# Splitting the odd maximum tile over both row halves, and exponentials over pairs of PSUM banks, in a fused attention and token-mixing kernel

## The chip, the cores and the metric

The kernel runs on one core of a Trainium2 chip. A core has five engines with queues of their own: TensorE (PE in the profile; its weight loads are shown apart as PEld), VectorE (DVE), ScalarE (ACT), GpSimd (POOL) and SyncE (SP, which only issues DMAs here). They meet through semaphores. Matmul results land in PSUM, which has eight banks of 512 float32 values per partition; everything else lies in SBUF or DRAM. The metric is the time of one execution on the device in microseconds (us), of which the median over several runs is given.

## The reference

Two branches work on the same input x (2048 tokens, 640 channels, float32), and a gate per token mixes them. What the change touches is the attention branch with 32 heads of width 20:

```python
qkv = (x @ wqkv).reshape(B, S, 3, H, Dh)            # transposed to q, k, v per head
scores = jnp.einsum("bhqd,bhkd->bhqk", q, k) * (Dh ** -0.5)
p = softmax(scores, axis=-1)
a = (jnp.einsum("bhqk,bhkd->bhqd", p, v) back to (B, S, D)) @ wo

h = layernorm(x)                                     # branch B: MLP over the token axis
u = gelu(jnp.einsum("bsd,sf->bdf", h, w1) + b1)
b = (jnp.einsum("bdf,fs->bds", u, w2) + b2) transposed to (B, S, D)

g = sigmoid((x * gate_w).sum(-1, keepdims=True))
out = g * a + (1 - g) * b
```

All of it has to hold to float32 accuracy, so most products are made of two rounded parts, high and low, in three matmuls.

## The kernel before

Heads are worked on in 16 pairs p. Head j of a pair (j = 0, 1) has its rows of q and k stacked in partitions 64j to 64j + 61, so a matmul of head 0 uses the upper 64 rows of the PE array and one of head 1 the lower 64 rows; the two row halves can work side by side.

The softmax needs the maximum over all 2048 keys of each query before the exponentials are made. So each pair is gone through twice. The first pass (the "s" tiles, line 178) computes scores with queries as output partitions, 128 queries by 512 keys, and DVE reduces each tile to one maximum per query (line 180). There are 128 such tiles per pair: two halves of the queries, eight blocks t of 128 queries, four blocks kc of 512 keys, two heads. When the tiles of a half are done, `s_max` reduces the four partial maxima (line 143), negates and splits them on POOL, and `s_store` transposes and stores them to DRAM; `load_m` brings them back as two more rows of the q stack. The second pass (the "st" tiles, line 700) computes the scores again, with keys as output partitions and with the negated maximum added by those rows. ACT makes the exponential (line 703), and "pv" matmuls (line 637) multiply it by v.

The stages are: projections; the MLP of branch B, between whose matmuls the first 736 maximum tiles are spread (the loop that calls `s_next`); the attention loop; and the output projection (lines 724 to 750).

The attention loop has 16 x 32 iterations. An iteration takes 128 keys (kt) and 1024 queries (qh) of a pair: four st tiles (head j, column block c), four exponentials, and the pv products of the iteration before (`pv_flush`). Between the st matmuls it deals out the remaining 1312 maximum tiles, `take` of them, three in 344 iterations, two in 140 and none in the last 28. The variable `turn` alternates the heads so that an st tile in one row half stands next to an s tile in the other. With three s tiles there are seven tiles of 512 columns for two row halves. After the last pv product of 16 iterations, DVE copies the accumulated pv tile out of PSUM (`pv_evac`, line 618), and POOL issues its stores.

The order on every engine is the order of the program here: scheduling is switched to manual for PE, ACT and DVE, and later for POOL and SP. An instruction that waits therefore holds back all that stand behind it on its engine.

PSUM is divided by tags: "st" has four buffers of one bank, "s" three and "pv" one, eight banks in all. Buffers of a tag are used in turn: a new tile lands in the buffer of the tile that many places before it and has to wait until that tile was read. Exponentials land in twelve SBUF tiles of 512 columns ("pt").

Of the kernel before, what the change touches and what calls it, by code (L numbers as in the profile page):

```python
# [7 lines left out]
F32 = mybir.dt.float32  # L8
F32R = mybir.dt.float32r
AF = mybir.ActivationFunctionType  # L10
OP = mybir.AluOpType
AX = mybir.AxisListType

P = 128
S, D, H, DH, F = 2048, 640, 32, 20, 1728
# [13 lines left out]
def gated_mix(ctx, tc, xT, x, wqk, wv0, wv1, wo, w1, w1t, b1, w2, b2, out):  # L29
    nc = tc.nc  # L30
    EG = mybir.EngineType
    ctx.enter_context(tc.manual_schedule(engines={EG.PE}))
    PSUM = bass.MemoryType.PSUM
    SCALE = DH ** -0.5

    def hi_lo(hi, lo, src, hi_eng=None, lo_eng=None):
        if hi_eng is nc.scalar:
            nc.scalar.activation(hi, src, AF.Copy)  # L38
        else:
            (hi_eng or nc.vector).tensor_copy(hi, src)  # L40
        (lo_eng or nc.vector).tensor_sub(lo, src, hi.bitcast(F32))  # L41
# [22 lines left out]
    cp = ctx.enter_context(tc.tile_pool(name="cp", bufs=1))  # L64
    base = ctx.enter_context(tc.tile_pool(name="base", bufs=1))
    psum = ctx.enter_context(tc.tile_pool(name="psum", bufs=1, space=PSUM))

    def st_tile(shape, name):
        return psum.tile(shape, F32, tag="st", bufs=4, name=name)

    def s_tile(shape, name):
        return psum.tile(shape, F32, tag="s", bufs=3, name=name)
# [44 lines left out]
    def base_stack(p, full, eng=nc.sync):  # L117
        ks = k8([P, S], F32R, f"ks{p}_{full}")
        qs = [q4([P, S // 2], F32R, f"qs{p}_{full}_{i}") for i in range(2)]
        load_stack(p, ks, qs, full, eng)  # L120
        return ks, qs

    def load_m(p, qs, half, put=nc.sync.dma_start):
        src = m_d[p, half].rearrange("(g i j t) r -> i j t g r", i=2, j=2, t=8)
        for j in range(2):
            for i in range(2):
                r = 64 * j + 3 * DH + i
                dst = qs[half].bitcast(F32)[r: r + 1, :].rearrange("o (t g r) -> o t g r", g=4, r=32)
                put(dst, src[i: i + 1, j])

    s_src, st_src, v_tiles = {}, {}, {}

    def load_v(p):
        v_tiles[p] = base.tile([P, NT, NPAIR], F32, tag="v", bufs=2, name=f"v{p}")
        c0 = NPAIR * (p % 8)
        nc.sync.dma_start(v_tiles[p], v_d[p // 8, :, :, c0: c0 + NPAIR].rearrange("t p c -> p t c"))

    s_close = []

    def s_max(p, half, mx):  # L140
        mm = cp.tile([P, 16], F32, tag="mm", bufs=2, name=f"mm{p}_{half}")
        mc = cp.tile([P, 32], F32R, tag="mc", bufs=2, name=f"mc{p}_{half}")
        nc.vector.tensor_reduce(mm, mx.rearrange("p k j t -> p (j t) k"), axis=AX.X, op=OP.max)
        nc.gpsimd.tensor_scalar_mul(mm, mm, -1.0)
        hi_lo(mc[:, :16], mc[:, 16:], mm, hi_eng=nc.gpsimd, lo_eng=nc.gpsimd)
        s_close.append([8, lambda: s_store(p, half, mc)])

    def s_store(p, half, mc):
        mt = cp.tile([P, 32], F32, tag="mt", bufs=2, name=f"mt{p}_{half}")
        nc.vector.transpose(mt, mc.bitcast(F32))  # L150
        s_close.append([M_LAG[0], lambda: m_queue[0].dma_start(m_d[p, half], mt)])

    M_LAG = [8]

    def s_next():
        next(stream)()
        for e in list(s_close):
            e[0] -= 1
            if e[0] <= 0:
                s_close.remove(e)  # L160
                e[1]()

    def s_finish():
        next(stream, None)
        while s_close:
            s_close.pop(0)[1]()

    def s_tiles(p):
        for half in range(2):
            mx = cp.tile([P, 4, 2, 8], F32, tag="mx", bufs=2, name=f"mx{p}_{half}")  # L170
            for t in range(8):
                for kc in range(4):
                    for j in (1, 0):
                        def f(j=j, kc=kc, t=t):
                            ks, qs = s_src[p]
                            ps = s_tile([P, 512], f"s{p}_{half}_{t}_{j}_{kc}")
                            r = slice(64 * j, 64 * j + 3 * DH)
                            nc.tensor.matmul(ps, qs[half][r, t * P:(t + 1) * P], ks[r, kc * 512:(kc + 1) * 512],  # L178
                                             start=True, stop=True)
                            nc.vector.tensor_reduce(mx[:, kc, j, t: t + 1], ps, axis=AX.X, op=OP.max)  # L180
                        yield f
            s_close.append([2, lambda p=p, half=half, mx=mx: s_max(p, half, mx)])

    def s_stream(on_start):
        for p in range(NP):
            on_start(p)
            yield from s_tiles(p)

    hooks = [None]
    m_queue = [nc.gpsimd]  # L190
    stream = s_stream(lambda p: hooks[0](p))

    p1s = ExitStack()
# [99 lines left out]
    for half in range(2):  # L293
        wvh, wvl = wvs[half]
        width = HALF + 2 if half == 0 else HALF
        for t in range(NT):
            n = NT * half + t
# [9 lines left out]
            ps = st_tile([P, width], f"v{half}_{t}")  # L307
# [256 lines left out]
    while done < S_AHEAD:  # L564
        s_next()
        done += 1
# [5 lines left out]
    lp = lps.enter_context(tc.tile_pool(name="lp", bufs=1, side="right"))  # L572

    def s_stack(p):
        ks = lp.tile([P, S], F32R, tag="sk", bufs=2, name=f"sk{p}")
        qs = [lp.tile([P, S // 2], F32R, tag="sq", bufs=4, name=f"sq{p}_{i}") for i in range(2)]
        load_stack(p, ks, qs, False)
        return ks, qs
# [66 lines left out]
    def load_wo(c):  # L645
        raw = ap.tile([P, D], F32, tag="wor", bufs=1, name=f"wor{c}")
        nc.gpsimd.dma_start(raw, wo[c * P:(c + 1) * P, :])
        hi_lo(woh[c], wol[c], raw, hi_eng=nc.gpsimd, lo_eng=nc.gpsimd)
# [15 lines left out]
    def o_early(q, hi_eng=nc.scalar, lo_eng=nc.vector):  # L664
        o_hl[q] = o_part(q, slice(0, (NC - 1) * P), NC - 1, 256, "e", 2, hi_eng, lo_eng)
# [1 line left out]
    def o_late(q):  # L667
        return o_part(q, slice((NC - 1) * P, D), 1, 512, "l", 4, nc.scalar, nc.vector)[0]

    turn = given = 0  # L670
    LEFT = NP * 128 - S_AHEAD
    for p in range(NP):
        ks, qs = st_src[p]
        if 8 <= p < 8 + NC:
            load_wo(p - 8)
        for it in range(32):
            qh, kt = divmod(it, NT)
            if p + 1 < NP:
                if it == 6:
                    st_src[p + 1] = base_stack(p + 1, True)  # L680
                if it == 12:
                    load_v(p + 1)
                if it == 27:
                    load_m(p + 1, st_src[p + 1][1], 0)
            if it == 11 and p:
                load_m(p, qs, 1)
            if it == 14 and due_stack:
                n = due_stack.pop()
                if n < NP:
                    s_src[n] = s_stack(n)  # L690
            if p == NP - 1 and it in (20, 26):
                o_early(it // 26, nc.gpsimd, nc.gpsimd)
            if kt == 0:
                pv = psum.tile([P, 512], F32, tag="pv", bufs=1, name=f"pv{p}_{qh}")
            pts = {}

            def st_op(j, c, tile):
                r = slice(64 * j, 64 * j + 3 * DH + 2)
                ps = tile([P, 512], f"st{p}_{it}_{j}{c}")
                nc.tensor.matmul(ps, ks[r, kt * P:(kt + 1) * P], qs[qh][r, c * 512:(c + 1) * 512],  # L700
                                 start=True, stop=True)
                pt = lp.tile([P, 512], F32, tag="pt", bufs=12, name=f"p{p}_{it}_{j}{c}")
                nc.scalar.activation(pt, ps, AF.Exp, scale=SCALE)  # L703
                pts[j, c] = pt

            due = min((p * 32 + it + 1) * LEFT // (NP * 32 - 28) + 1, LEFT)
            take = min(due - given, 3)
            for n in range(4):
                st_op((n + turn) % 2, n // 2, s_tile if n == 2 and take < 3 else st_tile)
                if n < take:  # L710
                    s_next()
            given += take
            if take and given == LEFT:
                s_finish()
            turn = (turn + take) % 2
            pv_flush()
            if p * 32 + it in later:
                later.pop(p * 32 + it)()
            pend.append((p, qh, kt, pv, pts))
    pv_flush()  # L720
    ordered.close()
    lps.close()

    ep = ctx.enter_context(tc.tile_pool(name="ep", bufs=1, side="right"))
    tys = [ep.tile([P, 2, HALF], F32, name=f"oy{t}") for t in range(NT)]
# [13 lines left out]
    for t in range(NT):  # L739
# [5 lines left out]
        ps = [st_tile([P, HALF], f"a{t}_{i}") for i in range(2)]  # L745
        a_mms(t, ps, o_hl[t // 2], slice((t % 2) * P, (t % 2 + 1) * P), range(NC - 1))
    for t in range(NT):
        ps = [st_tile([P, HALF], f"b{t}_{i}") for i in range(2)]
# [49 lines left out]
```

## Time and profile before

| | |
|---|---|
| time, median of 3 runs | 1844.79 us (1844.1 to 1847.46) |
| span of the profiled execution | 1844.8 us |
| attention loop, first to last pv weight load | 702.1 to 1762.6 us |
| PE, DVE, ACT busy over the span | 99%, 77%, 74% |
| PE clock granted | 1.00 of full speed in the loop |

Rows of the groups read: line, engine, operation, output and input with their partitions and elements, number of instructions; then busy time in us and the mean duration of one in ns; then the idle time before them and what ended it. Rows of the timeline read: start in us, length in us from the first start to the last end of the merged instructions, engine, line, operation, number of instructions, and in brackets the idle time before them with what ended it. A PE matmul without weights loaded ahead starts, in the records, together with its weight load. Durations of neighbours on DVE and ACT overlap, so the distance between two starts tells how many fit into a time.

### The profile page before, as it was taken

How to read it: one execution, taken by the hardware profiler on the slowest of the kernel's cores; microseconds unless marked ns; L12 is line 12 of the kernel's file. 1: busy time of each engine (PE TensorE's matmuls, PEld its weight loads, DVE VectorE, ACT ScalarE, POOL GpSimd, SP SyncE). 2: the span in 40 equal slices, each digit the busy share in tenths (PEclk: the TensorE clock that was granted, in tenths of full speed). 3: DMA queues.
4: the chain of work that ended last, by engine and by line, in shares of the span. 5: the costliest groups of instructions: out<-in, count | busy, mean ns of one | idle time of the engine just before them, and what ended most of it. 6: DMA issues, size and time to landing. Idle time of an engine off the chain costs nothing. (4 is left out here: it accounts for less than half of the span.)

```text
span 1844.8 us, 39129 instructions
## 1 busy us (share of the span) xinstructions
PE 1829.7 (99%) x14978; PEld 1135.2 (62%) x14978; DVE 1428.9 (77%) x2341; ACT 1361.6 (74%) x2688; POOL 637.1 (35%) x900
## 2 busy tenths in 40 slices
PE   9999999999999999999999999999999999999998
PEld 7998799999999994333333333333333333333378
DVE  4202299999999998888888888888888888888137
ACT  4243244465444448999999999999999999999930
POOL 1013478888887770112112111121321211212210
PEclk9999999999999999999999999999999999999999
DMA  8456766566645645504032324213540423301463
GB/s 289 143 169 212 222 173 173 158 194 193 168 139 166 189 136 121 118 15 103 20 85 61 73 42 93 57 50 78 107 103 24 109 47 77 71 14 23 131 219 132
DMA packets 152831, 216.61 MB, mean 117 GB/s; under 512 B 65698, under 2 KB 92082, under 8 KB 148738
## 3 DMA queue, kind: packets, MB, share of 16 engines
q1 hardware_dynamic: 129172, 178.68, 35.4%
q0 software_dynamic: 14688, 20.78, 5.2%
q10 hardware_dynamic: 8784, 14.65, 2.4%
q8 instruction: 118, 1.93, 0.4%
q14 instruction: 69, 0.57, 0.1%
HBM read 165.43 MB, written 48.25 MB: 116 GB/s over the span
## 5 line engine op out<-in xcount | busy, mean ns | idle before, releaser
L180 DVE TENSOR_REDUCE mx<-s 128x1 f32<-128x512 f32 x2048 | 1293.7, 684 | 159.9 <-PE s L178 119.7
L703 ACT ACTIVATE p<-st 128x512 f32<-128x512 f32 x2048 | 1042.1, 615 | 20.9 <-PE s L178 2.2
L700 PEld LDWEIGHTS st<-qs_True,ks_True 62*128 62x128 f32 x2048 | 307.3, 185 | 485.1 <-ACT p L703 312.9
L700 PE MATMUL st<-qs_True,ks_True 62*128 62x512 f32 x2048 | 579.6, 425 | 0.2 <-ACT ty L477 0.2
L637 PE MATMUL pv<-p,v 128*32 128x512 f32 x4096 | 555.5, 605 | 0.2
L178 PE MATMUL s<-sk,sq 60*128 60x512 f32 x1280 | 423.1, 434 | 0.0
L41 POOL TENSOR_TENSOR wl<-wr,wh 128x512 fp32r<-128x512 f32 x228 | 273.6, 1216 | 59.8 <-ACT wh L38 30.9
L624 POOL DMA_DIRECT2D o_d<-oev x128 | 67.0, 524 | 494.3 <-DVE oev L618 491.6
L178 PE MATMUL s<-ks_False,qs_False 60*128 60x512 f32 x768 | 225.1, 397 | 0.4 <-DVE mx L180 0.3
L46 PE MATMUL y<-gh,wh 64*128 64x320 f32 x896 | 216.8, 308 | 0.0
L46 PE MATMUL y<-gl,wh 64*128 64x320 f32 x832 | 210.3, 306 | 0.0
L46 PE MATMUL y<-gh,wl 64*128 64x320 f32 x832 | 209.4, 305 | 0.0
L38 ACT ACTIVATE wh<-wr 128x512 fp32r<-128x512 f32 (+2 forms) x246 | 135.9, 594 | 90.2 <-PE s L178 29.0
L178 PEld LDWEIGHTS s<-sk,sq 60*128 60x128 f32 x1280 | 197.7, 185 | 1.2
L637 PEld LDWEIGHTS pv<-p,v 128*32 128x32 f32 x4096 | 84.9, 108 | 171.4 <-issue 156.4
L46 PE MATMUL u<-hl,wh 64*128 64x320 f32 x864 | 167.1, 306 | 0.0
L46 PE MATMUL u<-hh,wh 64*128 64x320 f32 x864 | 167.1, 306 | 0.0
L46 PE MATMUL u<-hh,wl 64*128 64x320 f32 x800 | 156.9, 306 | 0.4 <-POOL wl L41 0.4
L46 PEld LDWEIGHTS y<-gh,wh 64*128 64x128 f32 x896 | 155.3, 184 | 0.4
L46 PEld LDWEIGHTS y<-gh,wl 64*128 64x128 f32 x832 | 147.0, 184 | 0.3
L46 PEld LDWEIGHTS y<-gl,wh 64*128 64x128 f32 x832 | 146.9, 184 | 0.0
L178 PEld LDWEIGHTS s<-ks_False,qs_False 60*128 60x128 f32 x768 | 124.4, 184 | 1.1 <-DVE mx L180 1.1
(124 smaller groups left out, 1817.6 us busy)
## 6 DMA issues: line engine op xcount, KB each, us to landing
wr<-in_w_dram SPq DMA_DIRECT2D x196, 256.0 KB
ks_True<-k_d SPq DMA_DIRECT2D x96, 160.0 KB
qs_True<-q_d SPq DMA_DIRECT2D x192, 80.0 KB
sk<-k_d SPq DMA_DIRECT2D x60, 160.0 KB
sq<-q_d SPq DMA_DIRECT2D x120, 80.0 KB
v_d<-vt SPq DMA_DIRECT2D x32, 168.0 KB
v<-v_d SPq DMA_DIRECT2D x16, 336.0 KB
xr<-in_xT_dram SPq DMA_DIRECT2D x20, 256.0 KB
```

The source lines that it names most:

```text
L38: nc.scalar.activation(hi, src, AF.Copy)
L41: (lo_eng or nc.vector).tensor_sub(lo, src, hi.bitcast(F32))
L46: nc.tensor.matmul(ps[k], a[r], b[r], start=start, stop=stop)
L178: nc.tensor.matmul(ps, qs[half][r, t * P:(t + 1) * P], ks[r, kc * 512:(kc + 1) * 512], start=True, stop=True)
L180: nc.vector.tensor_reduce(mx[:, kc, j, t: t + 1], ps, axis=AX.X, op=OP.max)
L624: nc.gpsimd.dma_start(o_d[DH * h: DH * h + DH, cols], ev[r: r + DH, :])
L637: nc.tensor.matmul(pv[r: r + 32, :], v_tiles[p][:, kt, 10 * j: 10 * j + 32], pts[j, c], start=(kt == 0), stop=(kt == NT - 1))
L700: nc.tensor.matmul(ps, ks[r, kt * P:(kt + 1) * P], qs[qh][r, c * 512:(c + 1) * 512], start=True, stop=True)
L703: nc.scalar.activation(pt, ps, AF.Exp, scale=SCALE)
```

## The change

- The odd third s tile of an iteration is replaced by two tiles of 128 queries by 256 keys, one of each head, of the same query and key block. Head 0's is the iteration's first matmul, head 1's the last one ahead of pv. They are halves (h = 0, 1) of the key blocks kc = 2 and 3; another iteration takes the other half. Full tiles of kc = 0 and 1 that are passed over on the way are taken later (`s_skipped`).
- The maxima therefore have six places per query instead of four. A full tile of kc = 2 or 3 is reduced as two segments of 256 in one instruction, in the MLP stage too. `s_max` reduces six values in place of four.
- The two full s tiles of an iteration stand together between the two st pairs; the order of heads is fixed (`turn` is gone).
- In the loop the four st banks become two tiles of two banks ("sp"): one for each column block c, with both heads side by side. One exponential covers both banks, 1024 columns, and writes a pt tile of 1024 (six buffers). In an iteration with an odd number of s tiles the first pair (c = 0) is still made by two exponentials of 512.
- The st pool is closed ahead of the loop and opened again behind it.

The number of s buffers stays at three.

```diff
-        next(stream)()
+        if not s_one:
+            s_one.extend(s_full(s_skipped.pop(0) if s_skipped else next(stream)))
+        s_one.pop(0)()
+        s_tick()
...
+    def s_full(u):
+        def f(j):
+            ps = s_tile([P, 512], f"s{u.p}_{u.half}_{u.t}_{j}_{u.kc}")
+            u.mm(ps, j, 0, 512)
+            if u.kc < 2:
+                nc.vector.tensor_reduce(u.mx[:, u.kc, j, u.t: u.t + 1], ps, axis=AX.X, op=OP.max)
+            else:
+                nc.vector.tensor_reduce(u.mx[:, 2 * u.kc - 2: 2 * u.kc, j, u.t],
+                                        ps.rearrange("p (a b) -> p a b", a=2), axis=AX.X, op=OP.max)
+            u.ended(2)
+        return [lambda j=j: f(j) for j in (1, 0)]
+
+    def s_half():
+        while not s_rest:
+            u = next(stream)
+            if u.kc < 2:
+                s_skipped.append(u)
+            else:
+                s_rest.extend([(u, 0), (u, 1)])
+        u, h = s_rest.pop(0)
+
+        def f(j):
+            ps = s_tile([P, 256], f"s{u.p}_{u.half}_{u.t}_{j}_{u.kc}_{h}")
+            u.mm(ps, j, 256 * h, 256)
+            nc.vector.tensor_reduce(u.mx[:, 2 * u.kc - 2 + h, j, u.t: u.t + 1], ps, axis=AX.X, op=OP.max)
+            u.ended(1)
+
+        f(0)
+
+        def close():
+            f(1)
+            s_tick()
+
+        return close
...
+            sps = [pair_pool.tile([P, 2, 512], F32, tag="sp", bufs=2, name=f"st{p}_{it}_{c}") for c in range(2)]
+
+            def st_mm(c, j):
                 r = slice(64 * j, 64 * j + 3 * DH + 2)
-                ps = tile([P, 512], f"st{p}_{it}_{j}{c}")
-                nc.tensor.matmul(ps, ks[r, kt * P:(kt + 1) * P], qs[qh][r, c * 512:(c + 1) * 512],
+                nc.tensor.matmul(sps[c][:, j], ks[r, kt * P:(kt + 1) * P], qs[qh][r, c * 512:(c + 1) * 512],
                                  start=True, stop=True)
-                pt = lp.tile([P, 512], F32, tag="pt", bufs=12, name=f"p{p}_{it}_{j}{c}")
-                nc.scalar.activation(pt, ps, AF.Exp, scale=SCALE)
-                pts[j, c] = pt
+
+            def st_exp(c, apart):
+                pt = lp.tile([P, 2, 512], F32, tag="pt", bufs=6, name=f"p{p}_{it}_{c}")
+                for j in (slice(1, 2), slice(0, 1)) if apart else (slice(0, 2),):
+                    nc.scalar.activation(pt[:, j], sps[c][:, j], AF.Exp, scale=SCALE)
+                for j in range(2):
+                    pts[j, c] = pt[:, j]
...
-            for n in range(4):
-                st_op((n + turn) % 2, n // 2, s_tile if n == 2 and take < 3 else st_tile)
-                if n < take:
+            close = s_half() if take % 2 else None
+            for c in range(2):
+                for j in (1, 0):
+                    st_mm(c, j)
+                st_exp(c, close and c == 0)
+                if c == 0 and take > 1:
                     s_next()
+                    s_next()
+            if close:
+                close()
```

More of the change, by code (lines that the diff above doesn't have):

```diff
@@ L66, in gated_mix @@
     psum = ctx.enter_context(tc.tile_pool(name="psum", bufs=1, space=PSUM))
+    four = ExitStack()
+    banks = [four.enter_context(tc.tile_pool(name="four", bufs=1, space=PSUM))]
     def st_tile(shape, name):
-        return psum.tile(shape, F32, tag="st", bufs=4, name=name)
+        return banks[0].tile(shape, F32, tag="st", bufs=4, name=name)
     def s_tile(shape, name):
@@ L153, in gated_mix, with s_tick @@
     M_LAG = [8]
-    def s_next():
-        next(stream)()
+    def s_tick():
         for e in list(s_close):
@@ L161, in s_next @@
                 e[1]()
+    def s_next():
+        if not s_one:
+            s_one.extend(s_full(s_skipped.pop(0) if s_skipped else next(stream)))
+        s_one.pop(0)()
+        s_tick()
     def s_finish():
-        next(stream, None)
+        assert not s_one and not s_rest and not s_skipped
         while s_close:
             s_close.pop(0)[1]()
[L168 to L182, printed above, removed]
@@ new lines, in gated_mix, with __init__, mm, ended @@
+    s_one, s_rest, s_skipped = [], [], []
+    class Unit:
+        def __init__(self, p, half, t, kc, mx, left):
+            self.p, self.half, self.t, self.kc, self.mx, self.left = p, half, t, kc, mx, left
+        def mm(self, ps, j, lo, n):
+            ks, qs = s_src[self.p]
+            r = slice(64 * j, 64 * j + 3 * DH)
+            k0 = self.kc * 512 + lo
+            nc.tensor.matmul(ps, qs[self.half][r, self.t * P:(self.t + 1) * P], ks[r, k0: k0 + n], start=True,
+                             stop=True)
+        def ended(self, n):
+            self.left[0] -= n
+            if self.left[0] == 0:
+                s_close.append([2, lambda: s_max(self.p, self.half, self.mx)])
@@ L186, in s_stream @@
             on_start(p)
-            yield from s_tiles(p)
+            for half in range(2):
+                mx = cp.tile([P, 6, 2, 8], F32, tag="mx", bufs=2, name=f"mx{p}_{half}")
+                left = [128]
+                for t in range(8):
+                    for kc in range(4):
+                        yield Unit(p, half, t, kc, mx, left)
     hooks = [None]
@@ L668, in o_late @@
         return o_part(q, slice((NC - 1) * P, D), 1, 512, "l", 4, nc.scalar, nc.vector)[0]
-    turn = given = 0
+    four.close()
+    pairs = ExitStack()
+    pair_pool = pairs.enter_context(tc.tile_pool(name="pairs", bufs=1, space=PSUM))
+    given = 0
     LEFT = NP * 128 - S_AHEAD
@@ L695, in gated_mix @@
             pts = {}
-            def st_op(j, c, tile):
+            sps = [pair_pool.tile([P, 2, 512], F32, tag="sp", bufs=2, name=f"st{p}_{it}_{c}") for c in range(2)]
+            def st_mm(c, j):
                 r = slice(64 * j, 64 * j + 3 * DH + 2)
-                ps = tile([P, 512], f"st{p}_{it}_{j}{c}")
-                nc.tensor.matmul(ps, ks[r, kt * P:(kt + 1) * P], qs[qh][r, c * 512:(c + 1) * 512],
+                nc.tensor.matmul(sps[c][:, j], ks[r, kt * P:(kt + 1) * P], qs[qh][r, c * 512:(c + 1) * 512],
                                  start=True, stop=True)
-                pt = lp.tile([P, 512], F32, tag="pt", bufs=12, name=f"p{p}_{it}_{j}{c}")
-                nc.scalar.activation(pt, ps, AF.Exp, scale=SCALE)
-                pts[j, c] = pt
+            def st_exp(c, apart):
[4 more added lines that the diff above has]
+                    pts[j, c] = pt[:, j]
             due = min((p * 32 + it + 1) * LEFT // (NP * 32 - 28) + 1, LEFT)
             take = min(due - given, 3)
-            for n in range(4):
-                st_op((n + turn) % 2, n // 2, s_tile if n == 2 and take < 3 else st_tile)
-                if n < take:
+            close = s_half() if take % 2 else None
[4 more added lines that the diff above has]
+                if c == 0 and take > 1:
                     s_next()
+                    s_next()
+            if close:
+                close()
             given += take
@@ L714, in gated_mix @@
                 s_finish()
-            turn = (turn + take) % 2
             pv_flush()
@@ L721, in gated_mix @@
     ordered.close()
+    pairs.close()
     lps.close()
+    banks[0] = ctx.enter_context(tc.tile_pool(name="late", bufs=1, space=PSUM))
     ep = ctx.enter_context(tc.tile_pool(name="ep", bufs=1, side="right"))
```

## The prediction

> **What bounds the kernel now.** I read the page's engine totals first, then its costliest groups, then the same groups over 900 to 1700 us (the middle of the attention loop), and then single iterations in the timeline.
>
> ```profile
> span 1844.8 us, 39129 instructions
> PE 1829.7 (99%) x14978; PEld 1135.2 (62%) x14978; DVE 1428.9 (77%) x2341; ACT 1361.6 (74%) x2688; POOL 637.1 (35%) x900
> ...
> L703 ACT ACTIVATE p<-st 128x512 f32<-128x512 f32 x1540 | 785.4, 604 | 15.4 <-PE s L178 0.9
> L180 DVE TENSOR_REDUCE mx<-s 128x1 f32<-128x512 f32 x1044 | 660.4, 683 | 120.6 <-PE s L178 91.9 <-PE st L700 26.4
> ```
>
> The last two rows are of the 800 us window. 1540 exponentials are 385 iterations, so an iteration takes 2.078 us on average; 1044 maxima are 2.71 per iteration, that is 71% iterations with three maximum tiles ("threes") and 29% with two ("twos"). ACT looks full (785 of 800 us), DVE waits for PE for most of its idle time. Which engine really sets the period is seen in single iterations, here the PE rows of a three (from 1201.71), the start of the next, and of a two (from 1210.15):
>
> ```profile
> 1201.71 0.50 PE L700 MATMUL st<-qs_True,ks_True 62*128 62x512 f32 x1
> 1202.05 0.40 PE L700 MATMUL st<-qs_True,ks_True 62*128 62x512 f32 x1
> 1202.28 0.40 PE L700 MATMUL st<-qs_True,ks_True 62*128 62x512 f32 x1
> 1202.52 0.39 PE L700 MATMUL st<-qs_True,ks_True 62*128 62x512 f32 x1
> 1202.84 1.07 PE L637 MATMUL pv<-p,v 128*32 128x512 f32 x8
> 1203.84 0.49 PE L700 MATMUL st<-qs_True,ks_True 62*128 62x512 f32 x1
> 1203.84 0.50 PE L178 MATMUL s<-sk,sq 60*128 60x512 f32 x1
> ...
> 1210.15 0.50 PE L700 MATMUL st<-qs_True,ks_True 62*128 62x512 f32 x1
> 1211.05 1.07 PE L637 MATMUL pv<-p,v 128*32 128x512 f32 x8
> 1212.05 0.49 PE L700 MATMUL st<-qs_True,ks_True 62*128 62x512 f32 x1
> ```
>
> A three is four slots, each holding one matmul in either row half (score in one, maximum in the other): 0.34, 0.23, 0.24, 0.32, then pv 1.00; 2.13 in all. The first slot has 0.10 of weight loading that nothing hides, the last 0.09 to 0.10 of changing over to pv. In the fourth slot one row half is empty. A two is three slots and pv, 1.90. No step of either holds a wait: the loop is bound by PE's own sequence. From the average, a three is (2.078 - 0.29 x 1.90) / 0.71 = 2.15 us.
>
> ```profile
> 1204.37 1.09 ACT L703 ACTIVATE p<-st 128x512 f32<-128x512 f32 x2
> 1204.86 1.57 ACT L703 ACTIVATE p<-st 128x512 f32<-128x512 f32 x3
> 1202.55 1.87 DVE L180 TENSOR_REDUCE mx<-s 128x1 f32<-128x512 f32 x3
> 1203.74 1.35 DVE L180 TENSOR_REDUCE mx<-s 128x1 f32<-128x512 f32 x2
> 1204.40 1.29 DVE L180 TENSOR_REDUCE mx<-s 128x1 f32<-128x512 f32 x2
> ```
>
> ACT's exponentials start (1.57 - 0.60) / 2 = 0.48 apart though one lasts 0.60, so four need 1.92: the busy share overstates ACT, which has 0.2 to spare in a three and none in a two. DVE's maxima start (1.87 - 0.68) / 2 = 0.60 apart: three need 1.79.
>
> **The change, part by part.** From here "s1, s0" are the full maximum tiles of a three, "h0" and "h1" its two halves. The new PE order of a three is h0, score pair c=0, s1, s0, score pair c=1, h1, pv. There are 344 threes (1312 maxima to give out in 484 iterations: 344 x 3 + 140 x 2) and 140 twos, then 28 iterations without maxima.
>
> *Row halves.* Each half gets 3.5 tiles in place of 4 and 3. Whether a short matmul lets the next one of its half start early is told by the earlier MLP stage, where 320-column and 512-column matmuls mix:
>
> ```profile
> 450.03 0.30 PE L46 MATMUL y<-gh,wh 64*128 64x320 f32 x1
> 450.10 0.31 PE L46 MATMUL y<-gl,wh 64*128 64x320 f32 x1
> 450.17 0.39 PE L178 MATMUL s<-ks_False,qs_False 60*128 60x512 f32 x1
> 450.25 0.31 PE L46 MATMUL y<-gh,wl 64*128 64x320 f32 x1
> ```
>
> The starts alternate 0.07 to 0.08 apart, less than the 0.15 that one 320-column matmul takes in its half: the halves do run skewed. The Trainium skill, "TensorEngine Tiling (Array Packing)", Key Properties, says that different tiles can load weights and multiply in parallel; these rows agree. So, by PE alone, h1 could start 0.34 + 0.23 + 0.23 = 0.80 after the start, and pv 0.11 (256 columns at the 0.23 / 512 of a slot) and 0.10 later: 1.01 in place of 1.15. That is 0.14 x 344 = 48 us of gain, if nothing waits.
>
> *The wait that comes with it.* There are three s buffers, and a three now takes four: h0, s1, s0, h1. h1 therefore lands in the buffer of h0 of the same iteration, and PE must wait until DVE has reduced h0. Before, three tiles per iteration met a buffer that was a whole period old. When is h0 reduced?
>
> ```profile
> 1204.47 0.19 PEld L700 LDWEIGHTS st<-qs_True,ks_True 62*128 62x128 f32 x2 [0.34 <-DVE mx L180]
> 1204.91 0.16 PEld L637 LDWEIGHTS pv<-p,v 128*32 128x32 f32 x8 [0.25 <-issue]
> ...
> L618 DVE COPY oev<-pv 128x512 f32<-128x512 f32 x32 | 21.9, 683 | 39.9 <-PE pv L637 39.9
> L315 DVE COPY gs<-v 128x2 f32<-128x2 f32 x16 | 2.5, 159 | 28.9 <-ACT vt L312 28.9
> ```
>
> (1) First-slot maximum to its reduction: 1203.84 to 1204.40, 0.56; for 256 columns 0.11 less, 0.45. (2) The reduction of 256: copies from PSUM cost (683 - 159) / 510 = 1.03 ns per column, so 0.68 - 0.26 = 0.42. (3) Release to PE: the reduction from 1203.74 ended at 1203.74 + 0.68 = 1204.42 and the weight load that waited for it began at 1204.47: 0.05. So h1's weight load starts 0.92 after the iteration's start. (4) The weights of a matmul that waits are not loaded ahead: that pair of full width needed 1204.91 - 1204.47 = 0.44 to pv, a half 0.33. pv starts at 1.25 and the iteration ends at 2.25, in place of 2.15. **344 x 0.10 = +34 us.** The skew gives nothing back, as h1 is last before pv. Each of (1) to (4) is good to about 0.02, so the three lies between 2.20 and 2.28: +17 to +45. If h1 did not wait at all: -48.
>
> The Trainium skill, same page, Instruction Overhead, puts some 60 cycles on every matmul and so speaks against splitting one; at a column per cycle (0.43 ns, from 0.23 against 0.15 us for 512 against 320 columns) that is 0.026 us, by an estimate +9 us for 344 more matmuls if it were exposed. The same two rows leave 0.01 us per matmul, and here it disappears in the wait.
>
> *Evacuation of pv.* DVE copies pv every 16 iterations, 0.60 between starts, 0.24 after the next iteration's start:
>
> ```profile
> 1201.95 0.68 DVE L618 COPY oev<-pv 128x512 f32<-128x512 f32 x1
> ```
>
> Before, this delayed no matmul of that iteration (1201.71 to 1203.84 is 2.13). Now it holds DVE from 0.24 to 0.84, so h0's reduction starts at 0.84 instead of 0.45 and h1 comes 0.39 later. 30 evacuations fall among maxima, 71% of them into a three: **+8 us** (0 to +12).
>
> *Exponentials.* ACT's one 1024-wide shape is a copy from SBUF:
>
> ```profile
> L38 ACT ACTIVATE wh<-wr 128x512 fp32r<-128x512 f32 x196 | 116.0, 625 | 65.2 <-PE s L178 29.0 <-POOL ty L481 18.1 <-DMA wr<-in_w_dram 11.9
> L38 ACT ACTIVATE ohe<-ore 128x1024 fp32r<-128x1024 f32 x6 | 6.4, 1061 | 30.8 <-PE a L732 30.8
> ```
>
> The second 512 columns cost 0.44, against 0.48 for a separate exponential. A two falls from 1.92 to 1.84 of ACT, a three (whose first pair stays two instructions) to 1.88. PE needs 1.90 and 2.25, so this gains nothing: I take 0 (to -2 us). The price is that a pair's buffer comes free only after the whole 1.04 us exponential. After a two, pair c=1 is released 0.53 + 0.92 + 1.04 + 0.05 = 2.54 after that two's start, 0.64 into the next iteration, where PE would reach it at 0.57: with its weights it streams at 0.74, h1 could follow at 0.97, which is no later than the 1.02 that the wait for h0 gives already. Cost 0, and 0.17 x 140 = 24 us if that cover were gone.
>
> *Last 28 iterations.* They have no maxima and take 1.96 now:
>
> ```profile
> 1728.26 0.73 PE L700 MATMUL st<-qs_True,ks_True 62*128 62x512 f32 x4
> 1730.22 0.73 PE L700 MATMUL st<-qs_True,ks_True 62*128 62x512 f32 x4
> ```
>
> PE alone would need about 1.66, but with two pair buffers PE waits for each whole exponential in turn; I come to iterations between 1.7 and 2.2, on average about as before. 0 (-8 to +3).
>
> *Maxima in the MLP stage.* Half of the 736 early ones now reduce two segments of 256.
>
> ```profile
> 300.00:700.00 400.00, 393.66 (x626) 1.00 0.57 164
> L143 DVE TENSOR_REDUCE mm<-mx 128x16 f32<-128x64 f32 x32 | 8.1, 253 | 0.0
> ```
>
> These rows are L180's DVE time in that stage, and the only reduction with many segments. Its 253 ns are 159 and 64 x 1.03 = 66, and 28 over for 16 segments. One more segment costs 0 to 0.03 us; 313 of them are at most 9 us of DVE, against 400 - 626 x 0.60 = 24 us unclaimed between the starts. 0 (to +6). The last reduction over 6 in place of 4 partial maxima, the reopened PSUM pools (one drain each) and loads that start up to two units of work earlier: 0 to 2 us together; the DMAs are the same in number.
>
> Sum, against the profiled 1844.8 us (the median of the runs is 1844.79): +34 + 8 = +42, **1887 us**.
>
> **Rivals.**
> A, faster: h1 does not really wait. It decides at 0.82: if h0 is released 0.10 us earlier than (1) to (3) say, a three costs what it did, and 0.2 us earlier the full gain of the row halves comes in. Then 2.01 per three, 1844.8 - 48 = 1797. For it: the skewed rows at 450 us. Against it: the three measured terms would have to shrink by a tenth together for break-even, by a fifth for the whole gain.
> B, ACT becomes the bound: long exponentials don't overlap their successors. Then a two takes at least 2 x 1.04 = 2.08, +0.18 x 140 = 25, and the tail about 3 more: 1915. Against it: starts 0.48 apart at 0.60 each.
> C, the row halves don't overlap in the new order, so the change doesn't do what it says. A three keeps four slots, h1 could start at 0.80, still before 0.92: again 1887, with other rows in the trace.
> D, the wait is half of what I think: +0.04 x 344, 1844.8 + 14 = 1859, or break-even.
>
> **How the numbers follow.** My forecast with C has 0.79; A 0.11; B 0.05; D 0.05, of which 0.02 is no change. From no change a measurement of this kernel tells about 0.2%, 1841 to 1848.5. The range runs from the short end of the three without the evacuations (+17, 1862) to its long end with evacuations and MLP segments (+45 + 12 + 6, 1908). Slower 0.87, same 0.02, faster 0.11.
>
> **What the trace after would show.** Right: h1's weight load in a three waits for DVE, starting 0.92 after h0's; threes of 2.25, twos of 1.90; pv 0.33 after h1's load; ACT idle grows to 0.3 a three. Wrong: h1's matmul at 0.80 and threes near 2.0 (A); twos over 2.0 with PE waiting for ACT (B); a score matmul of c=0 starting with s1 only after both halves are empty (C). The prediction fails first if the reduction of 256 columns is much cheaper than 0.42, or if its release reaches PE before its recorded end.

## The result and the profile after

The changed kernel takes 1886.51 us (median of 4 runs, 1885.29 to 1888.32), the kernel before on the same chip 1844.44 us (1843.97 to 1847.46). The ratio is 1.0224, 95% interval 1.0206 to 1.0242: slower by about 42 us, where 1887 us was forecast.

The first rows are from the page of the changed kernel, the rows behind the dots from its groups over 900 to 1700 us, the window that the prediction used.

```profile
span 1884.6 us, 40589 instructions
PE 1860.4 (99%) x15322; PEld 1160.0 (62%) x15322; DVE 1458.7 (77%) x2685; ACT 1333.2 (71%) x2008; POOL 636.7 (34%) x900
...
L754 PE MATMUL st<-qs_True,ks_True 62*128 62x512 f32 x1484 | 393.3, 458 | 0.1
L217 DVE TENSOR_REDUCE mx<-s 128x1 f32<-128x256 f32 x527 | 220.7, 419 | 66.7 <-PE s L185 65.7
L185 PEld LDWEIGHTS s<-sk,sq 60*128 60x128 f32 x1268 | 179.2, 185 | 261.7 <-DVE mx L198 134.1 <-DVE mx L200 71.3 <-DVE mx L217 20.8
L200 DVE TENSOR_REDUCE mx<-s 128x2 f32<-128x512 f32 x240 | 155.3, 687 | 20.8 <-PE s L185 20.8
```

1484 score matmuls in 800 us are 371 iterations, 2.156 us each; before it was 2.078. PE's busy share is 99% in both, which again says nothing: while one matmul waits inside an iteration, the records of its neighbours cover the time. The row of the weight loads of s tiles shows a wait that was not there, for the halves' maxima (L217, 20.8 us); the longer times behind L198 and L200 are mostly pv standing between the s tiles of two iterations. A reduction of two segments costs 687 ns where the one of a single segment cost 683 to 685, so the MLP stage kept its length: its last matmul starts at 698.5 us, before at 698.2.

Now one three (from 1204.82) and the two behind it (from 1207.03) in the timeline of the changed kernel, PE and its weight loads first, then DVE and ACT (the last row names the form of its first exponential; its second is the 1024-wide one of c=1):

```profile
1204.82 0.38 PE L185 MATMUL s<-sk,sq 60*128 60x256 f32 x1
1204.82 0.61 PE L754 MATMUL st<-qs_True,ks_True 62*128 62x512 f32 x2
1205.16 0.51 PE L185 MATMUL s<-sk,sq 60*128 60x512 f32 x2
1205.72 0.18 PEld L185 LDWEIGHTS s<-sk,sq 60*128 60x128 f32 x1
1206.03 0.16 PEld L686 LDWEIGHTS pv<-p,v 128*32 128x32 f32 x8
1207.03 0.49 PE L754 MATMUL st<-qs_True,ks_True 62*128 62x512 f32 x2
1207.59 0.19 PEld L754 LDWEIGHTS st<-qs_True,ks_True 62*128 62x128 f32 x2 [0.27 <-ACT p L760]
1208.02 0.16 PEld L686 LDWEIGHTS pv<-p,v 128*32 128x32 f32 x8 [0.24 <-issue]
1209.02 0.38 PE L185 MATMUL s<-sk,sq 60*128 60x256 f32 x1
...
1205.24 0.42 DVE L217 TENSOR_REDUCE mx<-s 128x1 f32<-128x256 f32 x1 [0.24 <-PE s L185]
1205.53 1.09 ACT L760 ACTIVATE p<-st 128x512 f32<-128x512 f32 x2 [0.20 <-PE st L754]
1206.03 1.51 ACT L760 ACTIVATE p<-st 128x512 f32<-128x512 f32 x2
```

In the three, h0 is issued at 1204.82, DVE reduces it from 1205.24 to 1205.66, h1's weights are loaded at 1205.72, pv starts at 1206.03 and the iteration ends after 2.21 us. In the two, no s tile waits; but the weights of its c=1 pair are loaded only at 1207.59, 0.56 after its start, when the wide exponential of the three before (the second of the last row, which ends at 1206.03 + 1.51 = 1207.54) has let go of that pair's banks. pv follows at 0.99 instead of 0.90, and the two takes 1.99 instead of 1.90.

An evacuation of pv, in the three that starts at 1219.83:

```profile
1219.97 0.69 DVE L667 COPY oev<-pv 128x512 f32<-128x512 f32 x1
1220.58 0.41 DVE L217 TENSOR_REDUCE mx<-s 128x1 f32<-128x256 f32 x1
1221.05 0.18 PEld L185 LDWEIGHTS s<-sk,sq 60*128 60x128 f32 x1 [0.47 <-DVE mx L217]
1222.36 0.18 PEld L754 LDWEIGHTS st<-qs_True,ks_True 62*128 62x128 f32 x2 [0.84 <-ACT p L760]
```

The copy holds DVE when h0 is ready; h1 is loaded 1.22 after the start (1219.83) in place of 0.90, and this three takes 2.53 us.

From the starts of the first matmul of every iteration in the two traces come the means (in brackets the medians) in us; the first two iterations, threes, and the last one are left out:

| | before | after | iterations x difference of means |
|---|---|---|---|
| threes | 2.149 (2.132) | 2.231 (2.207) | 342 x 0.082 = 28.0 |
| twos | 1.913 (1.896) | 1.980 (1.987) | 140 x 0.067 = 9.4 |
| last ones, without maxima | 1.952 (1.961) | 2.023 (2.016) | 27 x 0.071 = 1.9 |

Together 39.3 of the 39.8 us between the two profiled spans (the medians of the runs are 42 us apart). The 21 threes with an evacuation last 2.53 on average and the others 2.21, where both took 2.15 before. Of the threes' 28.0, 342 x 0.06 = 21 are thus what every three pays, and 21 x 0.32 = 7 what the evacuations add.

### The profile page after: what moved, and what is told of

Read it like the earlier page. It is cut to its first block, busy times and chain, and to the rows that moved or that the text cites. A ratio compares the mean times of both kernels' runs of the same rounds, so it can differ in the third digit from the quotient of the medians.

```text
span 1884.6 us, 40589 instructions
## 1 busy us (share of the span) xinstructions
PE 1860.4 (99%) x15322; PEld 1160.0 (62%) x15322; DVE 1458.7 (77%) x2685; ACT 1333.2 (71%) x2008; POOL 636.7 (34%) x900
## 5 line engine op out<-in xcount | busy, mean ns | idle before, releaser
L760 ACT ACTIVATE p<-st 128x512 f32<-128x512 f32 (+1 forms) x1368 | 1013.3, 810 | 88.3 <-PE st L754 66.3
L198 DVE TENSOR_REDUCE mx<-s 128x1 f32<-128x512 f32 x1024 | 659.4, 685 | 52.1 <-PE s L185 50.3
L754 PE MATMUL st<-qs_True,ks_True 62*128 62x512 f32 x2048 | 540.3, 460 | 4.4 <-ACT p L760 2.8
L185 PE MATMUL s<-sk,sq 60*128 60x512 f32 (+1 forms) x1614 | 460.3, 383 | 2.5 <-DVE mx L217 0.2
L200 DVE TENSOR_REDUCE mx<-s 128x2 f32<-128x512 f32 x680 | 436.5, 687 | 29.8 <-PE s L185 27.4
L185 PEld LDWEIGHTS s<-sk,sq 60*128 60x128 f32 x1614 | 228.4, 185 | 332.8 <-DVE mx L198 171.0
L754 PEld LDWEIGHTS st<-qs_True,ks_True 62*128 62x128 f32 x2048 | 228.3, 184 | 241.1 <-ACT p L760 218.0
L217 DVE TENSOR_REDUCE mx<-s 128x1 f32<-128x256 f32 x688 | 288.1, 419 | 86.6 <-PE s L185 85.3
L185 PE MATMUL s<-ks_False,qs_False 60*128 60x512 f32 (+1 forms) x778 | 242.4, 393 | 1.2 <-DVE mx L198 1.1
L46 PE MATMUL u<-hl,wh 64*128 64x320 f32 x864 | 189.6, 306 | 0.0
```

The costliest lines, as they stand in the source:

```text
L46: nc.tensor.matmul(ps[k], a[r], b[r], start=start, stop=stop)
L185: nc.tensor.matmul(ps, qs[self.half][r, self.t * P:(self.t + 1) * P], ks[r, k0: k0 + n], start=True, stop=True)
L198: nc.vector.tensor_reduce(u.mx[:, u.kc, j, u.t: u.t + 1], ps, axis=AX.X, op=OP.max)
L200: nc.vector.tensor_reduce(u.mx[:, 2 * u.kc - 2: 2 * u.kc, j, u.t], ps.rearrange("p (a b) -> p a b", a=2), axis=AX.X, op=OP.max)
L217: nc.vector.tensor_reduce(u.mx[:, 2 * u.kc - 2 + h, j, u.t: u.t + 1], ps, axis=AX.X, op=OP.max)
L754: nc.tensor.matmul(sps[c][:, j], ks[r, kt * P:(kt + 1) * P], qs[qh][r, c * 512:(c + 1) * 512], start=True, stop=True)
```

## The experiments

Two waits could make the loop longer: h1's for the reduction of h0 (W), and that of a score pair for the exponential of 1024 over its two banks. The experiments take out one of the two, the other, or both. Kernels that were run together share the runs of the kernel before: 1846.43 us for (1), (2), (4) and (5), 1847.54 us for (3), (6), (7) and (8).

**1. Without the maxima over h0.**

```diff
-            nc.vector.tensor_reduce(u.mx[:, 2 * u.kc - 2 + h, j, u.t: u.t + 1], ps, axis=AX.X, op=OP.max)
+            if j != 0:
+                nc.vector.tensor_reduce(u.mx[:, 2 * u.kc - 2 + h, j, u.t: u.t + 1], ps, axis=AX.X, op=OP.max)
...
                 mx = cp.tile([P, 6, 2, 8], F32, tag="mx", bufs=2, name=f"mx{p}_{half}")
+                nc.gpsimd.memset(mx, -30.0)
```

> The changed kernel without the 344 DVE maxima over h0 (the first half-tile of a three), so that h1 meets a buffer that nobody has to read; all matmuls stay. The values are wrong where h0 holds the maximum. Theory W1 (the wait for h0 is the only thing that keeps a three from 2.01 us): threes fall from 2.21 to 2.01, the 0.3 us per evacuation goes too, 1886 - 0.20 x 344 - 8 = 1810 us. Theory W2 (behind it stands the release of the c=1 pair): the wide exponential of a three ends 2.72 after the three's start, and PE then needs 0.05 + 0.10 of load + 0.23 + 0.11 + 0.10 + 1.00 to the end of the next iteration, so two iterations in a row take 4.31: threes of 2.15, twos somewhat longer than now, 1867 us. Theory X (h0 is not what h1 waits for, more work on DVE is): no more than the 344 x 0.33 us of DVE matter, threes stay at 2.2, 1880 to 1886 us.

Measured: 1910.02 us, ratio 1.0342 (1.0327 to 1.0358). Slower than every theory had it, and for a reason of the experiment: the filling stands on POOL's queue, which is long in the MLP stage, and DVE waits for it. By the profile DVE waits for it 15 times, 35 us in all, the longest time 6.0 us. A stretch of the MLP stage in this kernel (length, then PE, PEld, DVE, ACT, POOL busy with their instructions, then the granted PE clock, the DMA share and GB/s):

```profile
400.00:500.00 100.00, 93.30 (x1131) 92.03 (x1129) 88.04 (x146) 53.91 (x111) 80.98 (x89) 0.97 0.61 174
```

The same stretch in the changed kernel:

```profile
400.00:500.00 100.00, 100.00 (x1264) 99.55 (x1264) 98.43 (x161) 57.15 (x120) 87.52 (x93) 1.00 0.66 188
```

The MLP stage ends 27 us later, and a few iterations early in the loop take 3 to 6 us. The median three takes 2.156 us, as W2 has it; the total decides nothing, so the run was made again without that fault (3).

**2. Without the maxima over h1.** The edit of (1) with the other head, `if j != 1`, with the same fault.

> The changed kernel without the 344 DVE maxima over h1 instead: as much DVE work is left out as in the run without the maxima over h0, but h1 still waits for h0. W1 and W2: threes stay at 2.21, 1883 to 1887 us. X (DVE's load): the same time as the run without the maxima over h0.

Measured: 1931.95 us, ratio 1.0461 (1.0444 to 1.0478). Here too the MLP stage ends 29 us late and some iterations of the loop are long, so the total decides nothing. By the median, which the long ones hardly move, a three of the loop takes 2.207 us to the changed kernel's 2.207, and h1 waits as before:

```profile
1204.94 0.18 PEld L185 LDWEIGHTS s<-sk,sq 60*128 60x128 f32 x1 [0.84 <-DVE mx L198]
1205.84 0.18 PEld L185 LDWEIGHTS s<-sk,sq 60*128 60x128 f32 x1 [0.15 <-DVE mx L218]
1206.15 0.16 PEld L688 LDWEIGHTS pv<-p,v 128*32 128x32 f32 x8
```

From h0's load to h1's it is 0.90 though every three has one reduction of 0.42 us less on DVE. DVE's load (X) is not the cause; which tile's reduction is missing decides.

**3. Without the maxima over h0, filled on DVE.**

```diff
+                if 2 * p + half > 10:
+                    nc.vector.memset(mx[:, 2:], -30.0)
```

> As the first run without the maxima over h0, but the unwritten places of the maxima are filled by DVE ahead of the loop's groups only, not by POOL in every group, since that filling held up the MLP stage and some iterations. W1: threes 2.01, 1810 us. W2: threes 2.15 with PE waiting for the wide exponential ahead of the c=1 pair, twos 2.02, no long evacuation iterations: 1867 us. X: 1880 us or more.

Measured: 1865.60 us, ratio 1.0100 (1.0083 to 1.0117). W2, to 2 us. Threes have a mean of 2.155, twos 2.014, and the threes with an evacuation (2.17) are hardly longer than the others. Two threes in a row and the start of the next, weight loads of h0, of the c=1 pair, of h1 and of pv:

```profile
1203.73 0.18 PEld L185 LDWEIGHTS s<-sk,sq 60*128 60x128 f32 x1 [0.84 <-DVE mx L200]
1204.42 0.19 PEld L757 LDWEIGHTS st<-qs_True,ks_True 62*128 62x128 f32 x2 [0.28 <-ACT p L763]
1204.53 0.19 PEld L185 LDWEIGHTS s<-sk,sq 60*128 60x128 f32 x1
1204.96 0.16 PEld L689 LDWEIGHTS pv<-p,v 128*32 128x32 f32 x8 [0.24 <-issue]
1205.96 0.18 PEld L185 LDWEIGHTS s<-sk,sq 60*128 60x128 f32 x1 [0.84 <-DVE mx L198]
1206.50 0.19 PEld L757 LDWEIGHTS st<-qs_True,ks_True 62*128 62x128 f32 x2
1206.61 0.19 PEld L185 LDWEIGHTS s<-sk,sq 60*128 60x128 f32 x1
1207.05 0.16 PEld L689 LDWEIGHTS pv<-p,v 128*32 128x32 f32 x8 [0.25 <-issue]
1208.04 0.18 PEld L185 LDWEIGHTS s<-sk,sq 60*128 60x128 f32 x1 [0.84 <-DVE mx L198]
```

h1 is now loaded 0.11 after the c=1 pair, without a wait. The c=1 pair is loaded 0.69 after the first start, waiting for ACT, and 0.54 after the second. The two threes last 2.23 and 2.08, 4.31 together as W2 had worked out. So h1's wait, taken away by itself, gives back about half of the 42 us (21 between the two medians, 24 when each is compared with the kernel before of its own runs); behind it the pair's release is the next limit.

**4. The split alone.** The pair tiles are undone; order and maxima stay.

```diff
-                nc.tensor.matmul(sps[c][:, j], ks[r, kt * P:(kt + 1) * P], qs[qh][r, c * 512:(c + 1) * 512],
+                sps[c, j] = st_tile([P, 512], f"st{p}_{it}_{j}{c}")
+                nc.tensor.matmul(sps[c, j], ks[r, kt * P:(kt + 1) * P], qs[qh][r, c * 512:(c + 1) * 512],
...
+                for j in (1, 0):
+                    pt = lp.tile([P, 512], F32, tag="pt", bufs=12, name=f"p{p}_{it}_{j}{c}")
+                    nc.scalar.activation(pt, sps[c, j], AF.Exp, scale=SCALE)
```

> The odd tile split as in the changed kernel, in the same PE order, but four st tiles of one bank with four exponentials of 512 each. If h1's wait is the price in threes and the pair's late release the price in twos: threes stay at 2.21, twos fall from 1.98 to 1.91, the 28 last iterations from 2.02 to 1.95: 1886 - 0.07 x 140 - 2 = 1875 us. If the wide exponentials cost nothing: 1886 us. If they are what makes the threes long: below 1850 us.

Measured: 1873.43 us, ratio 1.0154 (1.0137 to 1.0171). Threes 2.228 (median 2.206), twos 1.898; the last iterations 2.04. The first branch holds: in the changed kernel the threes' price is the split's, the twos' price the pairs'. The expected gain in the last iterations did not come.

**5. The pairs alone.** The third maximum tile is whole again and stands behind the c=1 pair.

```diff
-            close = s_half() if take % 2 else None
...
-                st_exp(c, close and c == 0)
+                st_exp(c, take == 3 and c == 0)
...
-            if close:
-                close()
+            if take == 3:
+                s_next()
```

> Pairs of banks and exponentials of 1024 as in the changed kernel (threes with two of 512 for c=0), but the odd third maximum tile whole, behind the c=1 pair. If h1's wait is the price in threes: threes return to 2.14 to 2.15, the c=1 pair is released at 2.63 after the start and read at 0.49 of the next, so twos are 1.92: 1847 us. If the pair's late release costs 0.07 in every two whatever stands in a three: 1856 us. If the pairs lengthen the threes: 1870 us or more.

Measured: 1878.32 us, ratio 1.0175 (1.0159 to 1.0190). The third branch: without any half-tile the threes take 2.213 on average. A three behind a two (from 1205.55) and the three behind it (from 1207.88):

```profile
1205.55 0.18 PEld L754 LDWEIGHTS st<-qs_True,ks_True 62*128 62x128 f32 x2 [0.84 <-ACT p L760]
1206.23 0.18 PEld L754 LDWEIGHTS st<-qs_True,ks_True 62*128 62x128 f32 x2 [0.38 <-ACT p L760]
1206.88 0.16 PEld L686 LDWEIGHTS pv<-p,v 128*32 128x32 f32 x8 [0.36 <-issue]
1207.88 0.19 PEld L754 LDWEIGHTS st<-qs_True,ks_True 62*128 62x128 f32 x2 [0.84 <-ACT p L760]
1208.22 0.19 PEld L754 LDWEIGHTS st<-qs_True,ks_True 62*128 62x128 f32 x2
```

In the first the c=1 pair waits for ACT until 0.68 after the start, and the iteration takes 2.33; in the second it doesn't wait. So it is over all iterations: leaving out those with an evacuation, threes behind a two take 2.31 on average (2.17 before), threes behind a three 2.15 (2.14 before). The price is paid in the 131 threes behind a two, 131 x 0.14 = 18 us: that is the case without cover that the prediction had put at 24 us. The new order of the tiles stays in this run; single banks in that order with a whole third tile were not tried. Each half of the change thus costs most of the loss by itself, 27 us (4) and 32 us (5), and both together only 42: the waits stand beside each other in the same iterations.

**6. Neither wait.** The split alone, without the maxima over h0 (edits of 3 and 4).

> Split alone (four st tiles of one bank, four exponentials of 512), and again without the maxima over h0. Neither h1's wait nor the pair's release is there. The fourth exponential of a three ends 2.59 after its start; the st tile that reuses its buffer gives P = 2.59 + 0.05 + 0.10 + 0.32 + 1.00 - P, so threes of 2.03, twos of 1.90, 1805 us, if W2 holds and the row halves overlap as in the MLP stage. If the row halves gave nothing in this order, threes would be 2.13 and the time 1840 us.

Measured: 1832.81 us, ratio 0.9921 (0.9907 to 0.9936). Between the two branches: threes 2.057, but twos 2.021. The halves of the array do run skewed in this order, since threes fall below the 2.13 of four slots. What holds them now is ACT and the release of its buffers. ACT's row over 900 to 1700 us, then the timeline of a two (from 1205.54), with the last exponential of the three before and the two's first one in one row, and the weight load of the two's last score:

```profile
L761 ACT ACTIVATE p<-st 128x512 f32<-128x512 f32 x1564 | 797.7, 604 | 2.6 <-PE st L755 0.3
...
1205.46 1.21 ACT L761 ACTIVATE p<-st 128x512 f32<-128x512 f32 x2
1206.13 0.18 PEld L755 LDWEIGHTS st<-qs_True,ks_True 62*128 62x128 f32 x1
```

1564 exponentials in 800 us are 0.51 each and 2.046 per iteration, whichever kind; the profile counts hardly any of ACT's time as idle. The first exponential of the ACT row ends, by its record, at 1206.08, and 0.05 later the weights of the two's last score are loaded: it lands in the bank that this exponential has just read. The trace shows these 0.05 in nearly every iteration, so the chain that the expectation had priced for threes (2.03) holds the twos as well, which it had put at 1.90. Even without the wait, the split would thus be worth 0.8%, not the 48 us that PE alone promises.

**7. and 8. All exponentials of 512, and all of 1024,** with pairs and halves as in the changed kernel.

```diff
-                st_exp(c, close and c == 0)
+                st_exp(c, True)
```

> The changed kernel with pairs of banks, but all exponentials of 512. If what counts of the pairs is when the last exponential of the c=1 pair ends: it ends at 2.76 instead of 2.72 after a three's start, twos get 0.04 longer, threes 0.03 to 0.04 (the c=1 pair then delays h1 beyond its wait for h0): 1900 us. If only h0's wait counts in threes: 1892 us. If the width of the exponential is what costs: 1875 us.

Measured: 1901.29 us, ratio 1.0299 (1.0282 to 1.0316).

```diff
-                st_exp(c, close and c == 0)
+                st_exp(c, False)
```

> The changed kernel with every exponential 1024 wide, those of c=0 in threes too. The last exponential of a three then ends at 2.69 instead of 2.72: threes stay at 2.21 by h0's wait, twos get 0.03 shorter, 1882 us. If the width of the exponential is what costs: 1895 us or more.

Measured: 1883.32 us, ratio 1.0198 (1.0183 to 1.0214). Both totals are as expected from the time at which the last exponential of a three ends. Twos are 2.041 with narrow and 1.932 with wide ones, threes 2.238 and 2.237. With narrow ones the threes did not get 0.03 to 0.04 longer as expected, and the twos lost 0.06 instead of 0.04. No cost of the width itself shows, as the all-wide kernel is the faster of the two; what costs is that two banks come free together and late.

## Why the prediction was right, and where it was not

The time came out within 1 us, partly by luck: two errors of opposite sign met, h1's wait 13 us smaller than forecast and a wait in the twos that the sum did not have. The terms as measured add up to 39; the rest of the 42 us lies within the scatter of the runs.

- *h1's wait, +34.* The mechanism was right and was shown: with h0's reduction gone the wait is gone (3), with h1's gone it is not (2). The four terms measured 0.42 (0.45 expected), 0.42 (0.42), 0.05 (0.05), and 0.31 to pv (0.33); a three takes 2.21, not 2.25, and the term is 21 us. The first and the last were 0.02 to 0.03 too long.
- *Evacuations, +8.* Measured 7: the 21 threes were right, each is 0.32 longer in place of 0.39.
- *Exponentials, 0.* This is the step that failed. It looked at a three behind a two, where h1's wait covers the pair's, and named 24 us for the case without cover, but did not look at a two behind a three. A two has no h1 and so no cover: 9 us. In threes the cover is there, but it is narrow: (3) shows the pair's release 0.05 us behind, (5) shows it alone costing more than h1's wait does. The kernel before already held a little of such a wait, against "no step of either holds a wait": its threes behind a two took 2.17, those behind a three 2.14, and in the three from 1212.05 the last score's weights are loaded at 1212.80, 0.05 after the last exponential of the two before it ended.
- *Last iterations, 0 (-8 to +3).* Measured +2. *MLP stage, 0.* Measured below 1. ACT's idle time in the three shown is 0.20 (the first of the ACT rows), not 0.3.
- *The row halves.* They run skewed, as the rows at 450 us had it. The Trainium skill's "TensorEngine Tiling (Array Packing)", Key Properties, that different tiles can load weights and multiply in parallel, is borne out: in (6) the skewed order takes threes to 2.06, below the 2.13 of four full slots.
- *Rival A, 1797.* Its price was wrong: with the wait gone and single banks the kernel takes 1833, since ACT's exponentials and the release of their buffers leave an iteration 2.05 on average. Its "full gain" treated PE as the only limit. *Rival B* (ACT without overlap) is refuted by the profile: the two exponentials in the last ACT row of the changed kernel, 0.59 and 1.03 long, end 1.51 after the first starts. *C* is refuted by (6), and by the changed kernel itself: in the three above head 0's score of c=0 ends 0.61 after the start, having begun 0.22 after it (a score that waits for nothing lasts 0.39 to 0.40), and s1 begins at 0.34, so the halves do not change over together.

That the c=1 release is the very next limit behind h1's wait was shown by (3). Whether a fourth s buffer would do the same as leaving out the reduction was not tried, as all eight banks are taken.

## What to carry to other kernels

Count the tiles of a step against the buffers of their tag before anything else: the first step that makes one tile more than there are buffers waits for a reader of its own iteration, and its price is a chain of producer, reader and release that can be summed from rows. A buffer that is joined from two comes free when the later of its halves has been read, and the sum has to be made for every kind of iteration behind every other kind, the short one behind the long one above all. Where two waits stand in one place, taking away either gives back less than it costs alone (here 27 and 32 us alone, 42 together), and their costs don't add.

## What was not expected of the hardware

An engine whose exponentials start 0.48 apart in a row did not get below 0.51 on average in (6), although by the profile's count it was idle for 2.6 of 800 us in all. The overlap of neighbours hides the gap: a start that comes 0.6 after the last one counts as no idle time, because the last one lasts 0.6. The trace shows where the gap sits. Within an iteration of (6) the exponentials start 0.48 to 0.49 apart, from the last one of an iteration to the first of the next it is 0.60 on average, and that first one starts 0.04 after the end of the iteration's first score. The iteration cannot start earlier because its predecessor's last score waited for ACT's release, as the rows of (6) show. So the gap is the return trip from ACT over the buffer's release and PE back to ACT. This is read from the trace; no run took the trip away.
